# A fused state-space scan and ELU feed-forward kernel: scan bursts, two block turns and the weight sums placed differently

## The chip, the cores and the metric

The kernel runs on one core of a Trainium2 chip. The core has TensorE (matrix products; PE in the profile, its weight loads PEld), VectorE (DVE), ScalarE (ACT), GpSimd (POOL) and SyncE (SP), which issues the transfers. The metric is device time in microseconds (us). The kernel before takes 362.3 us, the median of three runs (361.17 to 363.4).

## The reference

The first half is a Mamba-2 scan with 4 batches, 8 heads, 768 tokens, head width 32 and state width 16, in chunks of tokens. The second is a feed-forward layer with ELU over the 3072 x 256 result:

```python
cum = np.cumsum(np.log(np.clip(a, 1e-6, 1.0)))      # within a chunk
M = (C @ B.T) * exp(cum_i - cum_j) * causal
y = M @ x + (C @ state) * exp(cum)
state = exp(cum_last) * state + sum_j B_j x_j exp(cum_last - cum_j)
...
h = y @ w_in                                   # 3072x256 @ 256x2048
g = np.where(h > 0, h, np.exp(np.minimum(h, 0)) - 1)
out = g @ w_out                                # 3072x2048 @ 2048x256
```

The weights come as 64-bit floating-point numbers; the kernel makes 32-bit ones of their two halves of words.

## The kernel before, in words

**Blocks.** The 3072 tokens are 12 blocks of 256 (BLK). Block n belongs to a batch and a place in it; blocks 2p and 2p + 1 are a pair. Within a block the scan works in quarters of 64 tokens (u, v) and groups of two heads (q).

**The scan of a block** is a chain of steps, each a function: `load_bc` and `load_x` bring B, C and x; `turn` brings B and C into the layout with the state width down the partitions, by four TensorE transposes (L389), a ScalarE copy (L393) and a VectorE product with the mask `hmask2` (L396); `turn_exp` multiplies C by the decay `ec` (L404). From block 6 on the same is done without TensorE: `load_bc` loads B and C in squares and B once more token by token (`b_tok`), and `turn_part` runs, one part at a time, two VectorE transposes of 32 x 32 squares (`turn_square`, L413), the mask (`mask_heads`, L421) and `turn_exp`. `decay` fills L on ScalarE and GpSimd, `scaled` scales B on GpSimd (L379), `scores` are the products C B (L501), `weigh` multiplies them by L (L510), `sums` are the products B x (L531), `states` carries the state on (VectorE, then GpSimd), and `across` (L576) and `inside` (L595) are the products with the state and with M; ScalarE copies their result into yT (L612). The products of `scores`, `sums`, `across` and `inside` are small (32 or 64 rows) and many: a burst in TensorE's stream. For two blocks together `across` and `inside` are 96 products, which stand in the profile as 192 weight loads and 192 products, since each fp32 product is done in two halves.

**The layer.** `l1(n, i)` makes two of 16 column groups of h for block n (L625, four products of 128 x 256), `elu` turns them into g (ScalarE L638 and L645, VectorE L647), `l2(n, j)` adds up the output (L746). Blocks 0 to 3 use these for the first layer. From block 4 on, a pair goes through a seven-product scheme of the Strassen-Winograd kind: the pair's inputs and the weights are summed first (`sum_y` on GpSimd, `sum_weights`), `front`, `mid` and `back` are the seven products of one column group (L697) with VectorE sums between them (`front_sums` L714, then L722 and L730), and `second(n)` is the second layer of a pair, in 56 steps of two products each (L807), with `sum_t1`, `sum_t2` and `add` on GpSimd and VectorE. Its first user is the pair of blocks 2 and 3.

**Order.** Nothing is reordered: each engine does its instructions in the order in which the code issues them, and waits at semaphores. The order is written out by hand:

- a prologue for blocks 0 and 1, then twelve `l1` of blocks 0 and 1 (the loop at L966), with the scan of block 2 between them;
- stages 2 and 3 (the loop at L1082), eight steps each: `l2` of block n - 2, `l1` of block n, its ELU, the conversion of a piece of w_out (`w_take` and `w_give`, in the first six steps of stage 2), and parts of the scans of blocks 3, 4 and 5. In stage 3, `more_sums(i)` makes part i of the sums of both weights (VectorE for w_out, GpSimd for w_in, L673) and the sum `sum_t1` of the pair 2, 3 (L774);
- stages 4, 6, 8 and 10 (the loop at L1122), 16 steps k each, two per column group: even steps `front`, odd ones `mid` and `back`, with steps of `second(n - 2)` between them (`l2s`), and the scan of the next pair. `ends` says at which step the pair's `across` and `inside` come (`end_of_two`), `left` makes what is left of the weight sums, in steps of one VectorE instruction;
- `second` of the last pair, and the stores.

Rotating buffers set further waits: seven PSUM buffers in the pool `ps_a`, two each of `bc`, `b_tok` and `bct`.

Of the kernel before, what the change touches and what calls it, by code (L numbers as in the profile page):

```python
# [16 lines left out]
P = 128  # L17
Q = 64
BLK = 2 * P
# [9 lines left out]
def kernel(  # L29
# [27 lines left out]
    nc = tc.nc  # L57
# [48 lines left out]
    def load_bc(n, c_queue=nc.sync):  # L106
        b, g = place(n)
        st.setdefault(n, {})["bc"] = raw.tile([P, 2, 2, NH, N], F32, tag="bc", name="bc", bufs=2)
        if n > 5:
            st[n]["b"] = raw.tile([P, 2, NH, N], F32, tag="b", name="b_tok", bufs=2)  # L110
            for u in range(2):
                sl = slice((2 * g + u) * P, (2 * g + u + 1) * P)
                nc.sync.dma_start(
                    out=st[n]["b"][:, u], in_=B[b, :, sl, :].rearrange("h s n -> s h n"))


            squares = st[n]["bc"].rearrange("p k u h n -> p k (u h n)").rearrange(
                "p k (m r) -> p k m r", m=2)
            for k, src in enumerate((B, C)):
                for m in range(2):  # L120
                    nc.sync.dma_start(
                        out=squares[:, k, m],
                        in_=src[b, m:NH:2, g * BLK:(g + 1) * BLK, :].rearrange(
                            "q (c t) n -> q c (t n)", t=8))
            return
        for u in range(2):
            sl = slice((2 * g + u) * P, (2 * g + u + 1) * P)
            for k, src in enumerate((B, C)):
                (nc.sync, c_queue)[k].dma_start(
                    out=st[n]["bc"][:, k, u], in_=src[b, :, sl, :].rearrange("h s n -> s h n"))  # L130
# [243 lines left out]
    def scaled(n, eng):  # L374

        s = st[n]
        s["sc"] = sc = att.tile([P, 2, NH, N], F32, tag="sc", name="sc", bufs=2)
        factor = eb0[:, :, NH * n:NH * (n + 1)] if n < 2 else eb[:, :, rows_of(n)]
        eng.tensor_tensor(  # L379
            out=sc, in0=s["b"] if n > 5 else s["bc"][:, 0],  # L380
            in1=factor.unsqueeze(3).to_broadcast([P, 2, NH, N]), op=ALU.mult)

    def turn(n):
# [232 lines left out]

    g_of = {}

    def l1(n, i):

        ps = psum([P, 2, BLK], "ps_h")
        for j in range(2):
            m = 2 * i + j
            for k in range(KC):
                nc.tensor.matmul(  # L625
                    out=ps[:, j], lhsT=w_in[:, k, m * P:(m + 1) * P],
                    rhs=yT[n // 2][:, k, n % 2].rearrange("p u i -> p (u i)"),
                    start=(k == 0), stop=(k == KC - 1))
        lag.append((n, i, ps))

    lag = []
# [334 lines left out]
    for s, (n, i) in enumerate((  # L966
            (1, 0), (1, 1), (1, 2), (0, 4), (1, 3), (0, 5), (1, 4), (0, 6), (1, 5), (0, 7),
            (1, 6), (1, 7))):
        l1(n, i)
        if s < 8:  # L970
            decay_of(2, s)
        if s == 7:
            scores(2)
            weigh(2, 0)
            weigh(2, 1)
        if s % 2 == 1 and todo < 10:
            w_take(todo, nc.vector)
            w_give(todo)
            w_load(todo + 6)
            todo += 1  # L980
        if s == 4:
            scaled(2, nc.gpsimd)
        if s == 5:
            turn(2)
            first_exp(2)
            turn_exp(2)
        if s == 8:
            spread_cum(3)
            load_x(3)
            spread_exp(3)  # L990
            weigh(2, 2)
            weigh(2, 3)

            st[0] = kept
            sums(2, 0, pool=p_o, tag="o", parts=(None, last))
            states(0, last)
            st.pop(0)
            states(2)
        if s == 10:
            spread_cum(4)  # L1000
            inside(across(2), 2)
        if len(lag) > 1:
            elu()


    ends = {(3, 13): (4, 5), (4, 13): (6, 7), (6, 13): (8, 9), (8, 12): (10, 11)}

    def end_of_two(n, step):
        ns = ends.get((n, step))
# [9 lines left out]
    def scan_ahead(n, i):  # L1019


        m = n + 2 + n % 2
        if 4 < m < NP and n % 2 == 1 and i in (4, 5):
            spread_cum(m + i - 4)
        m = n + 2 - n % 2
        if 4 <= m < NP and n % 2 == 0:
            if i < 2:
                if m == 4:
                    load_bc(m + i)
                spread_exp(m + i)  # L1030
            if i == 2:
                if m == 4:
                    spread_cum(5)
                load_x(m)
                load_x(m + 1)
            for k in (i,) if m == 4 else (i, i + 1) if i % 2 == 0 else ():
                if k >= 2:
                    decay(m + k // 6, (k - 2) % 4)
            if m == 4 and i in (5, 7):
                turn(m + i // 7)  # L1040
                turn_exp(m + i // 7)
        if n % 2 == 1 and i in (1, 3) and n + 3 + i // 2 < NP:
            load_bc(n + 3 + i // 2)
        if n == 3 and i > 3 and i < 7:
            turn_part(6, i - 4)
        if 4 <= m < NP and n % 2 == 1:
            if i == 0:
                scaled(m, nc.gpsimd)
                scaled(m + 1, nc.gpsimd)
            for k in (i,) if m == 4 else (i, i + 1) if i % 2 == 0 else ():  # L1050
                if k < 2:
                    decay(m + 1, k + 2)
            if i == 2 and m == 4:
                scores(m, m + 1)
                sums(m, m + 1)
                for q in range(4):
                    weigh(m, q)
                    weigh(m + 1, q)
                states(m)
                states(m + 1)  # L1060
# [15 lines left out]
    def more_sums(i):  # L1076
        sum_weights(nc.vector, a_out, s_out, i)
        sum_weights(nc.gpsimd, a_in, s_in, i)
        sum_t1(2, i, nc.vector)


    for n in (2, 3):  # L1082
        for i in range(8):
            l2(n - 2, i)
            if todo < len(pieces):
                w_take(todo, nc.vector)
# [25 lines left out]
            else:  # L1112
                if i == 0:
                    s_in[:], s_out[:] = weight_sums(), weight_sums()
                elif i < 7:
                    more_sums(i - 1)
            scan_ahead(n, i)
            end_of_two(n, 2 * i + 1)
    sum_t2(2, 0)
    left = (step for i in (6, 7) for step in weight_steps(nc.vector, a_out, s_out, i))  # L1120

    for n in range(4, NP, 2):  # L1122
        m = n + 2 if n + 2 < NP else None
# [13 lines left out]
        for k in range(16):  # L1137
# [16 lines left out]
                    end_of_two(n, k)  # L1154
                    l2s(2)
            elif m and i == 5:
                l2s(1)
                mid(n, i)
                begin_elu()
                states(m)  # L1160
# [5 lines left out]
            else:  # L1166
# [9 lines left out]
                begin_elu()  # L1176
                turn_step(n, k, True)
                if n == 4 and i < 4:
                    for _ in range(2):
                        next(left)()  # L1180
                    if i < 2:
                        sum_weights(nc.gpsimd, a_in, s_in, 6 + i)
                        sum_t1(2, 6 + i)
                l2s(1)
            if m:
                scan_ahead(n + k // 8, k % 8)
                if k == 9:
# [50 lines left out]
```

## Time and profile before

| | |
|---|---|
| timed runs, median (range) | 362.3 us (361.17 to 363.4) |
| the profiled execution, its own time | 363.81 us |
| its span, first to last instruction | 362.1 us |
| granted TensorE clock, mean | 0.993 |
| busy: PE, PEld, DVE, ACT, POOL | 352.8, 315.5, 240.4, 200.8, 232.0 us |
| products of `second` (L807), records x mean | 1120, 275 to 279 ns |
| products of `front`, `mid`, `back` (L697) | 448, 379 to 388 ns |
| products of `l1` (L625) | 256, 383 ns |
| HBM read and written | 22.12 and 3.34 MB |

The mean of a product is the time from its start to its modelled end; products are pipelined, so that the time from start to start is shorter. A row of a timeline or of the chain begins with the start and the length in us; x8 is the number of instructions merged into it; in brackets stands the idle time before it and what ended it. "issue" is time in which the engine waited for nothing that the profile shows.

### The profile page before, as it was taken

To read this page: it belongs to the slowest core of one execution; us is meant where nothing else is said; L and a number is where in the kernel's file an instruction comes from. 1 tells how busy PE (TensorE), PEld (TensorE's weight loads), DVE (VectorE), ACT (ScalarE), POOL (GpSimd) and SP (SyncE) were. 2 spreads that over 40 slices of the span, in tenths; PEclk is the share of its full clock that TensorE was granted. 3 is DMA by queue.
4 is the path that set the end of the run, shared out by engine and by line. 5 is a ranking of instruction groups with operands and counts; after the bars stand their busy time and mean duration, and the time that the engine had idled before them with its cause. 6 is when DMAs were issued, how large, how long until landed. Compare 5 with 4: busy or idle time off the path is not lost.

```text
span 362.1 us, 9921 instructions
## 1 busy us (share of the span) xinstructions
PE 352.8 (97%) x3954; PEld 315.5 (87%) x3954; DVE 240.4 (66%) x495; ACT 200.8 (55%) x493; POOL 232.0 (64%) x368
## 2 busy tenths in 40 slices
PE   8899999999999999999999999999979999999995
PEld 5578888888888998989999989999969999999995
DVE  3989978972699668675777575777564465556212
ACT  4759969767335666545676545676534443535000
POOL 5554544663467996868485968485966445465983
PEclk9999999999999999999999999999998999999999
DMA  8977998652350400155500164500000100000001
GB/s 169 207 206 153 230 292 169 109 81 45 73 119 31 89 0 3 24 119 112 101 0 2 23 129 102 102 3 0 2 2 4 58 2 1 2 0 31 30 2 58
DMA packets 85845, 26.09 MB, mean 72 GB/s; under 512 B 63848, under 2 KB 81704, under 8 KB 85800
## 3 DMA queue, kind: packets, MB, share of 16 engines
q1 hardware_dynamic: 83624, 25.27, 32.0%
q8 instruction: 31, 0.51, 0.6%
q10 hardware_dynamic: 2176, 0.20, 0.4%
q14 instruction: 14, 0.11, 0.1%
HBM read 22.12 MB, written 3.34 MB: 70 GB/s over the span
## 4 chain that ended last, share of the span: by engine, by line
PE 88%; POOL 5%; DVE 4%; issue 1%; ACT 1%; POOLq 0%; DVEq 0%
PE ps_o L807 32%; PE ps_h L697 25%; PE ps_h L625 14%; PE ps_o L746 8%; PE ps_y L595 2%; PE ps_g L501 2%; POOL g L762 2%; PE ps_y L576 1%; PE ps_st L531 1%; PE ps_idle L232 1%; POOL g L774 1%; DVE mag L207 1%; DVE mag L200 1%; POOL w_sum L673 1%; DVE M L510 1%
## 5 line engine op out<-in xcount | busy, mean ns | idle before, releaser
L638 ACT ACTIVATE e<-ps_h 128x512 f32<-128x512 f32 x96 | 57.0, 593 | 92.1 <-DVE ps_h L722 45.4
L807 PEld LDWEIGHTS ps_o<-w_out,g 128*128 128x128 f32 x640 | 80.3, 192 | 3.3 <-issue 0.5
L807 PE MATMUL ps_o<-w_out,g 128*128 128x128 f32 x640 | 81.4, 275 | 0.0
L647 DVE SCALAR_TENSOR_TENSOR g<-e,ps_h 128x512 f32<-128x512 f32 x96 | 65.0, 678 | 15.5 <-ACT e L645 15.1
L625 PE MATMUL ps_h<-yT,w_in 128*128 128x256 f32 x256 | 60.7, 383 | 2.0 <-POOL w_in L217 1.7
L645 ACT ACTIVATE e<-e 128x512 f32<-128x512 f32 x96 | 60.9, 635 | 2.0
L774 POOL TENSOR_TENSOR g<-g 128x256 f32<-128x256 f32 x34 | 25.1, 740 | 55.5 <-DVE g L647 55.5
L625 PEld LDWEIGHTS ps_h<-yT,w_in 128*128 128x128 f32 x256 | 47.7, 190 | 10.3 <-POOL w_in L217 3.1
L807 PE MATMUL ps_o<-w_sum,g 128*128 128x128 f32 x320 | 43.9, 279 | 0.0
L807 PEld LDWEIGHTS ps_o<-w_sum,g 128*128 128x128 f32 x320 | 41.9, 195 | 1.5 <-PE ps_y L595 0.2
L481 ACT ACTIVATE L<-L,ncum 128x64 f32<-128x64 f32 x160 | 41.0, 337 | 0.0
L697 PE MATMUL ps_h<-y_sum,w_sum 128*128 128x256 f32 x128 | 38.8, 384 | 0.5 <-DVE u_sum L714 0.5
L697 PE MATMUL ps_h<-yT,w_in 128*128 128x256 f32 x128 | 39.2, 388 | 0.0
L697 PE MATMUL ps_h<-y_sum,w_in 128*128 128x256 f32 x128 | 38.1, 380 | 0.0
L730 DVE TENSOR_TENSOR ps_h<-ps_h,u_sum 128x512 f32<-128x512 f32 x32 | 22.3, 698 | 23.6 <-PE ps_h L697 23.5
L486 POOL TENSOR_SCALAR_AFFINE_SELECT L<-L 64x512 f32<-64x512 f32 x40 | 28.1, 702 | 13.0 <-ACT L L481 11.7
L722 DVE TENSOR_TENSOR ps_h<-ps_h,u_sum 128x256 f32<-128x256 f32 x32 | 13.8, 431 | 30.5 <-PE ps_h L697 30.1
L714 DVE TENSOR_TENSOR u_sum<-ps_h,u_sum 128x512 f32<-128x512 f32 x32 | 22.0, 687 | 13.3 <-PE ps_h L697 8.0
L746 PE MATMUL ps_o<-w_out,g 128*128 128x256 f32 x128 | 30.8, 383 | 0.0
L762 POOL TENSOR_TENSOR t<-g 128x256 f32<-128x256 f32 x40 | 29.4, 767 | 0.3
L762 POOL TENSOR_TENSOR g<-g,t 128x256 f32<-128x256 f32 x40 | 28.7, 750 | 0.3
L697 PEld LDWEIGHTS ps_h<-y_sum,w_sum 128*128 128x128 f32 x128 | 24.2, 192 | 5.4 <-DVE u_sum L714 2.2
(111 smaller groups left out, 538.3 us busy)
## 6 DMA issues: line engine op xcount, KB each, us to landing
L<-flat SPq DMA_DIRECT2D x20, 256.0 KB, 6.6
w<-in_moe_w_in_dram SPq DMA_DIRECT2D x8, 512.0 KB
w<-in_moe_w_out_dram SPq DMA_DIRECT2D x8, 512.0 KB, 10.4
xr<-in_x_dram SPq DMA_DIRECT2D x24, 128.0 KB, 2.6
out_dram<-c_sum SPq DMA_DIRECT2D x10, 256.0 KB
bc<-in_B_dram SPq DMA_DIRECT2D x24, 64.0 KB, 5.7
bc<-in_C_dram SPq DMA_DIRECT2D x22, 64.0 KB
ec<-flat_exp SPq DMA_DIRECT2D x9, 128.0 KB
```

What stands on the lines that cost most here:

```text
L481: nc.scalar.activation(L[:, h, u], L[:, h, u], ACT.Exp, bias=ncum[:, u, row:row + 1])
L486: nc.gpsimd.affine_select(out=part, in_=part, pattern=[[0, 4], [0, 2], [1, Q]], compare_op=ALU.is_ge, fill=0.0, base=0, channel_multiplier=-1)
L625: nc.tensor.matmul(out=ps[:, j], lhsT=w_in[:, k, m * P:(m + 1) * P], rhs=yT[n // 2][:, k, n % 2].rearrange("p u i -> p (u i)"), start=(k = ...
L638: nc.scalar.activation(begun[0], lag[0][2], ACT.Relu, scale=-1.0)
L645: nc.scalar.activation(e, e, ACT.Exp, scale=-1.0)
L647: nc.vector.scalar_tensor_tensor(out=g_of[n, i], in0=e, scalar=1.0, in1=ps, op0=ALU.subtract, op1=ALU.max)
L697: nc.tensor.matmul(out=out, lhsT=lhsT, rhs=rhs, start=first, stop=True, skip_group_check=True)
L730: nc.vector.tensor_tensor(out=c2, in0=c2, in1=u[:, 0:2], op=ALU.add)
L746: nc.tensor.matmul(out=o_of[n][:, ts], lhsT=g_of[n, j][:, m % 2, ts * P:(ts + 1) * P], rhs=w_out[:, m], start=(m == 0 and ts == 0), stop=( ...
L762: nc.gpsimd.tensor_tensor(out=out, in0=in0, in1=in1, op=ALU.subtract)
L774: eng.tensor_tensor(out=b12, in0=b12, in1=b11, op=ALU.subtract)
L807: nc.tensor.matmul(out=ps[:, ts], lhsT=b[:, ts * P:(ts + 1) * P], rhs=a[:, i], start=(i == chunk[0] and ts == 0), stop=(i == chunk[-1]), s ...
```

## The change

- `l1` takes a number of parts; in the loop at L966 its first two calls (columns 0 and 1 of block 1) are issued with the 256 tokens in two halves, so that each of their products of 128 x 256 is two of 128 x 128.
- Blocks 4 and 5 take the path of the later blocks: loads in squares and `b_tok`, two VectorE transposes each, `mask_heads` and `turn_exp`, spread over steps 3 to 7 of stage 2 and steps 0, 2 and 3 of stage 3. Their TensorE transposes and ScalarE copies go.
- The end of blocks 10 and 11 moves from step 12 to step 13 of stage 8.
- In stage 3, `more_sums(i - 1)` is issued at the start of step i, ahead of that step's `l2`, `l1` and ELU, and for i up to 7; it stood after the ELU, for i up to 6. `left` holds only part 7, one instruction in each of four odd steps of stage 4, and GpSimd's part 6 and its `sum_t1` go from stage 4 into stage 3.
- In stages 4, 6 and 8 one step of `second` goes from step 9 (after `back`) to step 11 (before `mid`).

```diff
     def load_bc(n, c_queue=nc.sync):
-        if n > 5:
+        if n > 3:
             st[n]["b"] = raw.tile([P, 2, NH, N], F32, tag="b", name="b_tok", bufs=2)
...
-            out=sc, in0=s["b"] if n > 5 else s["bc"][:, 0],
+            out=sc, in0=s["b"] if n > 3 else s["bc"][:, 0],
...
-    def l1(n, i):
+    def l1(n, i, parts=1):
         ps = psum([P, 2, BLK], "ps_h")
         for j in range(2):
             m = 2 * i + j
-            for k in range(KC):
-                nc.tensor.matmul(
-                    out=ps[:, j], lhsT=w_in[:, k, m * P:(m + 1) * P],
-                    rhs=yT[n // 2][:, k, n % 2].rearrange("p u i -> p (u i)"),
-                    start=(k == 0), stop=(k == KC - 1))
+            for part in range(parts):
+                toks = slice(part * BLK // parts, (part + 1) * BLK // parts)
+                for k in range(KC):
+                    nc.tensor.matmul(
+                        out=ps[:, j, toks], lhsT=w_in[:, k, m * P:(m + 1) * P],
+                        rhs=yT[n // 2][:, k, n % 2].rearrange("p u i -> p (u i)")[:, toks],
+                        start=(k == 0), stop=(k == KC - 1))
...
-        l1(n, i)
+        l1(n, i, 2 if s < 2 else 1)
...
-    ends = {(3, 13): (4, 5), (4, 13): (6, 7), (6, 13): (8, 9), (8, 12): (10, 11)}
+    ends = {(3, 13): (4, 5), (4, 13): (6, 7), (6, 13): (8, 9), (8, 13): (10, 11)}
...
-            if m == 4 and i in (5, 7):
-                turn(m + i // 7)
-                turn_exp(m + i // 7)
+            if m == 4 and i > 2:
+                turn_part(m + i // 6, i % 3)
...
-        if n == 3 and i > 3 and i < 7:
+        if n == 3 and i == 0:
+            turn_part(5, 2)
+        if n == 3 and i in (2, 3):
+            turn_part(i + 2, 3)
+        if n == 3 and i in (4, 5, 6):
             turn_part(6, i - 4)
...
     for n in (2, 3):
         for i in range(8):
+            if n == 3 and i > 0:
+                more_sums(i - 1)
             l2(n - 2, i)
...
                 if i == 0:
                     s_in[:], s_out[:] = weight_sums(), weight_sums()
-                elif i < 7:
-                    more_sums(i - 1)
...
-    left = (step for i in (6, 7) for step in weight_steps(nc.vector, a_out, s_out, i))
+    left = weight_steps(nc.vector, a_out, s_out, 7)
...
             elif m and i == 5:
-                l2s(1)
+                l2s(2)
                 mid(n, i)
...
                 if n == 4 and i < 4:
-                    for _ in range(2):
-                        next(left)()
-                    if i < 2:
-                        sum_weights(nc.gpsimd, a_in, s_in, 6 + i)
-                        sum_t1(2, 6 + i)
-                l2s(1)
+                    next(left)()
+                    if i == 0:
+                        sum_weights(nc.gpsimd, a_in, s_in, 7)
+                        sum_t1(2, 7)
+                if not m or i != 4:
+                    l2s(1)
```

## The prediction

> **What bounds the kernel.** I read the page first (busy shares, slices, chain), then the waits of TensorE, then the chain in order of time, then the timelines of TensorE and VectorE around what stood out.
>
> ```profile
> PE 352.8 (97%) x3954; PEld 315.5 (87%) x3954; DVE 240.4 (66%) x495; ACT 200.8 (55%) x493; POOL 232.0 (64%) x368
> ...
> PE   8899999999999999999999999999979999999995
> ...
> PEclk9999999999999999999999999999998999999999
> ...
> q8 instruction: 31, 0.51, 0.6%
> ```
>
> TensorE is busy 97% and no other engine over 66%. One slice after the ramp falls to 7, the slice from 262.5 us, and the next one is the only one with a lower clock. The waits of TensorE name few causes:
>
> ```profile
> PE ps_y L595 <- issue: 1.8, 1, 1.8
> ...
> PE ps_h L697 <- DVE u_sum L714: 0.5, 1, 0.5
> ...
> PEld ps_h L697 <- DVE u_sum L714: 2.2, 5, 0.9
> ```
>
> So what can be won is TensorE's own work and these few gaps. The chain by time shows the big one:
>
> ```profile
> 171.79 1.30 PE ps_h L697 x6
> ...
> 226.09 1.30 PE ps_h L697 x6
> ...
> 266.70 0.89 PE ps_o L807 x8
> 269.48 1.81 issue
> 271.30 1.07 PE ps_y L595 x54
> 272.37 2.00 PE ps_o L807 x8
> ...
> 284.17 1.30 PE ps_h L697 x6
> ```
>
> 171.79, 226.09 and 284.17 are the first `front` of stages 6, 8 and 10. Stage 6 lasts 54.30 us, stage 8 58.08, with the same work but for 16 product records fewer in `sums` (0.86 against 0.72 us). Inside the burst of `across` and `inside` of blocks 10 and 11 TensorE waits 1.81 us for nothing but instructions, and right after it eight products take 2.00 us instead of 0.89. The window view has the cause of the second:
>
> ```profile
> 268.59:272.00 3.41, 1.59 (x133) 1.36 (x130) 0.56 (x2) 0.70 (x2) 2.82 (x4) 1.00 0.02 5
> 272.00:275.41 3.41, 3.41 (x37) 3.01 (x20) 0.00 (x0) 1.51 (x5) 2.42 (x4) 0.50 0.02 5
> ```
>
> (columns: stretch, its length, busy time of PE, PEld, DVE, ACT, POOL, then PEclk, DMA share, GB/s.) For 3.41 us the clock is halved.
>
> The instruction queue's packets tell where bursts run dry. Its 31 packets are 16,384 bytes each; TensorE has 8,011 records (each fp32 product of the program is two weight loads and two products). The wait at 269.27 comes before record 6593, the smaller one at 51.2 us (L625, 0.39 us) before record 1473: 5120 apart, 20 blocks of 256. So block starts lie at 193 + 256k, and in the quiet parts a packet starts from 2.5 us before to 1.1 us after TensorE enters the block ahead of it. The two-block bursts hold some 384 records in 2.4 us. The bad one begins 14 records after a block start, so 2.6 us later it needs the next block. That fetch began 2.28 us after the block was entered (why so late the trace doesn't show: no other packet moves then), took 0.93, and the record ran 1.43 us after it landed: 4.64 in all.
>
> **What the Trainium skill says.** "Runtime: NRT & Kernel Launch", Instruction fetch mechanics: instructions are refilled in blocks of 16 KiB, 256 instructions, and the crossing is mostly hidden. The trace agrees on size and count; hidden it is in 29 of 31. The same section gives TensorE room for 128 KiB; here the block needed was fetched only one block ahead. "TensorE: Matmul & The Clock Gate", Part 1: the clock halves after a window of about 3.4 us without enough activity. Here it did so for 3.41 us after a gap of 2 us inside a burst[...]. "VectorE: DVE Perf Modes", The three transpose paths: VectorE turns 32x32 blocks only, into SBUF. The trace has it at 638 ns for 128x256, which is why blocks 4 and 5 now need loads in squares and a second, token-wise load of B.
>
> **The change, part by part.** The sum is made against the profiled execution, 363.81 us (span 362.1 and 1.7 around it).
>
> *A, end of blocks 10 and 11 one step later.* It moves by 14 products, 56 records, and takes `sum_y` (four on POOL) with it; the next `front` is still two steps (6.15 us) away, as in stages 4 and 6. Counting the new order, the four two-block bursts begin 63, 59, 71 and 83 records after a block start (52, 47, 59 and 14 before): 8 products more are 32 records, 8 transposes less are minus 16, the rest are semaphore waits. At 0.11 us a record ahead of the burst the last is 83 x 0.11 + 1.1 = 10 us between block starts, and the shortest of the others 59 x 0.11 + 1.2 = 7.7, more than 4.64. The stall and the half clock go: 58.08 - 54.30 + 0.14 = 3.9. Minus 3.9.
>
> *B, blocks 4 and 5 turned by VectorE.*
>
> ```profile
> 75.45 0.38 PE L389 MATMUL ps_tb<-ident,bc 128*128 128x128 f32 x2
> 75.67 0.38 PE L389 MATMUL ps_tc<-ident,bc 128*128 128x128 f32 x2
> 75.89 1.89 PE L746 MATMUL ps_o<-w_out,g 128*128 128x256 f32 x8
> ```
>
> Each turn holds TensorE 0.44 us (75.45 to 75.89, again 84.22 to 84.66): minus 0.88. VectorE gains four squares (start to start 0.5), and two masks of 0.93 for 0.68: 2.5 us in all; ScalarE loses two copies (0.36 each), which nobody waited for. In stage 2 it has no idle until 79 us, so the last weight piece, which POOL finishes at 79.08, comes 1.0 later, 80.1; its `l2` starts at 80.67 - 0.44 = 80.23. Free, with 0.1 to spare; up to 0.3 if not. SP issues four loads more, about 2.4 us, ahead of x loads that end at 75.4 and are needed at 96; block 6's B waits for POOL's `scaled` at 88 and is needed at 109. Both nothing.
>
> *C, halved products.* 16 records at 216 ns (1.73 for eight) become 32 at 111 (1.78 for sixteen): plus 0.1. They move the block starts early too: record 1473 now falls 26 records before the end of block 2's burst, 0.8 us sooner. With the packet as before the wait grows by 0.9; with the packet 1.3 us earlier, since its block is entered sooner, it vanishes (minus 0.4). I take plus 0.3.
>
> *D, weight sums a step ahead.* Two things meet on VectorE where stage 4 begins:
>
> ```profile
> 118.25 0.69 DVE L647 SCALAR_TENSOR_TENSOR g<-e,ps_h 128x512 f32<-128x512 f32 x1 [0.37 <-PE ps_h L697]
> 118.86 0.68 DVE L714 TENSOR_TENSOR u_sum<-ps_h,u_sum 128x512 f32<-128x512 f32 x1
> ...
> 120.27 0.59 PE L697 MATMUL ps_h<-y_sum,w_sum 128*128 128x256 f32 x2
> ```
>
> The product at 120.27 waits for the sum that ends at 119.54: 0.7 to spare. Queued by hand with the durations of before (sums 2.3 to 2.9 for five, ELU 0.6, weighing 2.65, states 1.7), VectorE now has sums 0 and 1 in its idle time before 96 us, and from 100.9 on sums 2 to 6, five ELUs, two squares, a mask and a `cts`: the last ELU starts about 117.9 and `u_sum` ends at 119.2, against a product that is due at 119.5. The sums of part i - 1 wait for the products of step i - 1, which have read those weights; behind them stands the ELU of step i, and TensorE needs its buffer two steps later at the soonest. I take 0.2 lost, between 0 and 1. What it buys: POOL has one part of the sums less after 120 us and does it before `t`, so that the partial sum that VectorE awaited at 135.68 (1.30 us, POOL) comes 2 us sooner, and TensorE's gap at 138.5 (0.63) goes. Together minus 0.4.
>
> *E, one `l2` step from step 9 to step 11.* At 208.2 and twice more the second product of `mid` follows `u_sum` with one step (0.44) and one product between, and comes 0.14 late, with 0.10 more for the restart. One step more covers it: 3 x 0.24, minus 0.7. At step 9 nothing is uncovered, since the scores' buffers were freed by ELUs a step earlier.
>
> Sum: -3.9 - 0.9 + 0.1 + 0.3 - 0.4 - 0.7 = -5.5, so 358.3. The profiled execution lies 0.4 above the slowest timed run and 1.5 above the median (362.3), which a clock window that falls differently could explain. With the stall gone only the smaller offset should remain: 358.0, 1.2% under the median. About 1% is what this measurement can tell from no change.
>
> **Rivals.**
> 1. The dry fetch is not where but when: a late fetch meets another burst, or record 1473 costs its whole 1.3 us and a halved window (3.41 / 2 = 1.7): 358 + 3 = 361. For: the lateness at 268.93 has no visible cause. Against: the new distances exceed 4.64 everywhere else.
> 2. VectorE becomes the bound in stage 3. It is nine tenths busy from 99 to 117 us. If all seven groups take 2.9 as the last did rather than 2.45, it is 3.1 late, less 0.3 to spare: 360.8.
> 3. Slower: block starts lie otherwise than I count, within 40 records ahead of three or more bursts. Each then costs what blocks 10 and 11 cost now, 3.9; three make 358 + 11.7 = 369.7. It decides when my count is off by 20 to 60 records. Against: it rests on two stalls 20 blocks apart.
>
> The halving and the moves do stand in the built order, so that the change is not what it says is no case.
>
> **Numbers.** Forecast 0.63, rivals 0.18, 0.12, 0.07. Of the forecast nine tenths end under 358.7, plus a little of rival 2: faster 0.62; the rest of 1 and 2: same 0.31; slower 0.07. The range 356.4 to 361.4 takes in C and D at both ends and the first two rivals.
>
> **What would show it.** No issue wait over 0.3 us at an L595 after 60 us and no half clock after the ramp (A); stages of equal length; no L389 transposes for blocks 4 and 5 (B); no gap near 137 us (D); no `u_sum` wait after `sums` (E). Wrong if a PE wait on `u_sum` near 119 us exceeds 1 us, or an instruction wait stands in another burst.

## The result and the profile after

The changed kernel takes 357.8 us (median of four runs, 357.64 to 359.08) against 362.2 us for the kernel before beside it (361.17 to 363.4): the ratio is 0.9885, with a 95% interval from 0.9847 to 0.9923. A second measurement of it ("after, once more" in the table below, experiment 9) gave 357.8 us again. The profiled execution took 357.64 us with a span of 355.9 us, 6.2 us less than the one before. That is more than the medians show (4.4 us), and experiment 1 says why.

The page of the kernel after, its busy shares, the slices of TensorE and of its clock, and its instruction queue:

```profile
PE 349.0 (98%) x3962; PEld 313.4 (88%) x3962; DVE 242.5 (68%) x500; ACT 200.5 (56%) x491; POOL 231.8 (65%) x367
...
PE   8899999999999999999999999999999999999995
...
PEclk9999999999999999999999999999999999999999
...
q8 instruction: 31, 0.51, 0.6%
```

The 7 in the slices of TensorE and the 8 in those of the clock are gone, with the same 31 instruction packets. The waits of TensorE after (total us, times, longest us) are down to two lines, both from the ramp; no instruction wait and no wait for `u_sum` is left in them. In the list of the weight loads (PEld), one wait for `u_sum` of 0.2 us is left of the five:

```profile
PE ps_h L627 <- POOL w_in L217: 1.7, 3, 1.1
PE ps_idle L232 <- DVE idle L227: 1.1, 1, 1.1
...
PEld ps_h L699 <- DVE u_sum L716: 0.2, 1, 0.2
```

The chain of the kernel after, in order of time, with the first `front` of stages 6, 8 and 10 and the last two-block burst:

```profile
169.94 1.30 PE ps_h L699 x6
...
224.00 1.30 PE ps_h L699 x6
...
270.07 1.44 PE ps_y L595 x90
...
277.86 1.30 PE ps_h L699 x6
```

Stage 8 lasts 53.86 us where it lasted 58.08. The burst of blocks 10 and 11 (`inside`, L595) runs through in one piece of 1.44 us.

For all kernels below, the stages were also measured one way: from the first of the 64 products of a stage that read `y_sum` to that of the next. The first column of times says when stage 4 begins, which holds all that happens in the ramp and in stages 2 and 3. From there in stage 10 to the end of TensorE's last product it is 73.93 us in all of them.

| kernel | median us | stage 4 begins | stage 4 | stage 6 | stage 8 |
|---|---|---|---|---|---|
| before | 362.2 | 117.19 | 54.87 | 54.30 | 58.08 |
| after | 357.8 | 116.32 | 53.90 | 54.06 | 53.85 |
| after, once more | 357.8 | 116.69 | 53.90 | 54.06 | 53.85 |
| 1 before, once more | 362.5 | 118.35 | 54.91 | 54.30 | 55.92 |
| 2 only the end moved | 359.9 | 116.79 | 55.05 | 54.30 | 54.08 |
| 3 only products halved | 360.0 | 116.99 | 54.90 | 54.36 | 54.41 |
| 4 after, all twelve halved | 371.3 | 121.15 | 58.34 | 58.16 | 54.54 |
| 5 after, halves undone | 358.9 | 117.58 | 53.89 | 54.06 | 53.84 |
| 6 after, end undone | 358.0 | 116.72 | 53.89 | 54.06 | 54.17 |
| 7 after, sums undone | 359.2 | 116.34 | 54.92 | 54.06 | 53.84 |
| 8 after, l2 step undone | 359.0 | 116.95 | 54.13 | 54.33 | 54.08 |
| 10 after, turns undone | 359.0 | 118.48 | 53.90 | 54.25 | 53.89 |
| 11 after, three halved | 358.3 | 116.25 | 53.90 | 54.06 | 53.85 |

Where no instruction wait falls into them and nothing in them was changed, the stages repeat to 0.2 us, so they are the sharper measure. The start of stage 4 doesn't: the kernel before alone gave 117.19 and 118.35. Nor do the medians from row to row: experiments 1 to 4, 5 to 8 and 9 to 11 ran on three different chips, each group beside the kernel before, whose runs at the full clock had medians of 362.2, 362.1 and 363.0 us there. Only 10 and 11 stand beside the changed kernel (9). A difference of up to 1 us between the median of another row and 357.8 can be the chip's. In the group of 5 to 8, four of the seven runs of the kernel before had the half clock (experiment 1), which put its median at 364.3 us and makes the ratios given there too low.

### The profile page after: what moved, and what is told of

Its sections match the earlier page's. It is cut to its first block, busy times and chain, and to the rows that moved or that the text cites. A ratio compares the mean times of both kernels' runs of the same rounds, so it can differ in the third digit from the quotient of the medians.

```text
span 355.9 us, 9943 instructions
## 1 busy us (share of the span) xinstructions
PE 349.0 (98%) x3962; PEld 313.4 (88%) x3962; DVE 242.5 (68%) x500; ACT 200.5 (56%) x491; POOL 231.8 (65%) x367
## 4 chain that ended last, share of the span: by engine, by line
PE 93%; DVE 3%; ACT 1%; POOL 1%; issue 0%; POOLq 0%; DVEq 0%
PE ps_o L809 35%; PE ps_h L699 28%; PE ps_h L627 14%; PE ps_o L748 8%; PE ps_y L595 2%; PE ps_g L501 2%; PE ps_y L576 1%; PE ps_st L531 1%; PE ps_idle L232 1%; DVE mag L207 1%; DVE mag L200 1%; DVE M L510 1%; DVE sgn L192 0%; DVE g L649 0%; POOL w_in L217 0%; ACT L L471 0%
## 5 line engine op out<-in xcount | busy, mean ns | idle before, releaser
L627 PE MATMUL ps_h<-yT,w_in 128*128 128x256 f32 (+1 forms) x272 | 60.9, 371 | 1.7 <-POOL w_in L217 1.7
L776 POOL TENSOR_TENSOR g<-g 128x256 f32<-128x256 f32 x33 | 23.9, 726 | 54.4 <-DVE g L649 54.4
L809 PE MATMUL ps_o<-w_sum,g 128*128 128x128 f32 x320 | 42.9, 275 | 0.0
L809 PEld LDWEIGHTS ps_o<-w_sum,g 128*128 128x128 f32 x320 | 41.1, 192 | 1.2
L699 PE MATMUL ps_h<-yT,w_in 128*128 128x256 f32 x128 | 38.8, 385 | 0.0
L764 POOL TENSOR_TENSOR g<-t,g 128x256 f32<-128x256 f32 x40 | 27.9, 730 | 1.1 <-PE ps_o L809 1.1
```

The source lines that it names most:

```text
L627: nc.tensor.matmul(out=ps[:, j, toks], lhsT=w_in[:, k, m * P:(m + 1) * P], rhs=yT[n // 2][:, k, n % 2].rearrange("p u i -> p (u i)")[:, toks],
L699: nc.tensor.matmul(out=out, lhsT=lhsT, rhs=rhs, start=first, stop=True, skip_group_check=True)
L764: nc.gpsimd.tensor_tensor(out=out, in0=in0, in1=in1, op=ALU.subtract)
L776: eng.tensor_tensor(out=b12, in0=b12, in1=b11, op=ALU.subtract)
L809: nc.tensor.matmul(out=ps[:, ts], lhsT=b[:, ts * P:(ts + 1) * P], rhs=a[:, i], start=(i == chunk[0] and ts == 0), stop=(i == chunk[-1]), s ...
```

## The experiments

The first four put the cause of the long stage 8 to the test, four more undo one part of the change each in the changed kernel (a fifth follows as experiment 10), and two look at the ramp.

### 1. The kernel before, once more

No edit.

> The kernel before once more, without any edit. If the late fetch in the burst of blocks 10 and 11 is a property of where instruction blocks start in TensorE's stream, the profile has it again: an instruction wait of 1.5 to 2.5 us at an L595 near 270 us, stage 8 longer than stage 6 by 3.5 to 4.2 us, and a time within 0.5% of 362.2 us. If it was the chance of one execution, stage 8 is about 54.5 us here and the half clock is gone.

Median 362.5 us, ratio 1.000 (0.998 to 1.002). TensorE's timeline in the burst of blocks 10 and 11, and the clock slices of this execution:

```profile
268.72 1.24 PE L576 MATMUL ps_y<-cts,Sx 32*64 32x64 f32 x64
269.89 0.79 PE L595 MATMUL ps_y<-M,xr 64*32 64x64 f32 x56
271.95 0.96 PE L595 MATMUL ps_y<-M,xr 64*32 64x64 f32 x72 [1.27 <-issue]
...
PEclk9999999999999999999999999999999999999999
```

The instruction wait is there again, after the same 56 products of `inside`, but with 1.27 us where the first execution had 1.81, just under the range I gave, and with no half clock behind it. So stage 8 is 1.62 us longer than stage 6 here and was 3.78 us longer there. The wait belongs to the kernel; the half clock comes with it only sometimes. The granted clock of each timed run shows how often: of 70 runs of the kernel before, 27 have a mean clock of 0.989 to 0.995 and a median of 364.0 us, 43 have 0.998 or more and a median of 362.2. The difference, 1.8 us, is about half of the 3.41 us window. Of 48 timed runs of the kernels 2, 3 and 5 to 11, one is at a clock under 0.996, and so is one of the four of the changed kernel above (0.993, its slowest, 359.08 us); no profile of these two runs tells where.

The length of the wait need not be all that decides. In experiment 4, where the clock is halved three times, it changes at 116.15, 170.76 and 228.79 us: 16.0 and 17.0 times 3.413 us apart, as if on a fixed grid. In the execution of experiment 1 it changes once, after the last product, at 360.34 us; 26 such steps earlier is 271.60 us, which lies inside the wait. TensorE's busy time in the two stretches that share the wait stands behind the comma in each row:

```profile
268.18:271.60 3.42, 2.49 (x126) 2.00 (x125) 2.07 (x5) 0.96 (x3) 2.30 (x6) 1.00 0.02 5
271.60:275.01 3.41, 3.06 (x87) 2.86 (x87) 0.11 (x1) 1.84 (x5) 2.75 (x4) 1.00 0.02 5
```

That is 0.73 and 0.90 of a stretch, where the kernel before had its whole wait in one (268.59 to 272.00, busy 1.59 us, 0.47), and the half clock in the next. So a wait may bring the half clock or not by where it falls on the grid, which lies differently in every execution: whole in one stretch, this one would have left TensorE busy for 0.63 of it (1 - 1.27 / 3.41, an estimate). Whether that is little enough no run shows, nor that this parts the 27 runs from the 43: only two of the kernel's executions were profiled.

This is why the two profiles differ by more than the medians do: the profiled execution before was one of those with the half clock.

### 2. The end of blocks 10 and 11 alone

```diff
-    ends = {(3, 13): (4, 5), (4, 13): (6, 7), (6, 13): (8, 9), (8, 12): (10, 11)}
+    ends = {(3, 13): (4, 5), (4, 13): (6, 7), (6, 13): (8, 9), (8, 13): (10, 11)}
```

> Only the end of blocks 10 and 11 one step later; its burst now begins 71 records after a block start instead of 14. Theory (where the block starts fall): the instruction wait and the half clock of that burst go, stage 8 falls from 58.1 to 54.3 us, and the time falls by 3.9 us, to 358.3. Rival (the end a step later hands its sums on late, or other work waits): the wait stays or a wait on y_sum or w_sum stands before the first front of stage 10, 360 to 362.5 us. Rival (the profiled execution was an exceptional one, half of them have no half clock): 2 us less, 360.

359.9 us, ratio 0.9921 (0.9891 to 0.9951): 2.7 us less. Stage 8 is 54.08 us, 4.0 us under the first profile and 1.84 under the second. The mechanism is the theory's; the time is the second rival's (360), and the two don't exclude each other: the theory's 3.9 us was the size in an execution with the half clock. Against the 32 runs of the kernel before beside it, 12 of them at the half clock, the end is worth 2.7.

### 3. The halved products alone

```diff
-        l1(n, i)
+        l1(n, i, 2 if s < 2 else 1)
```

(with `l1` taking its parts as in the change)

> Only the halving of the first eight groups of first-layer products, which adds 32 product records (64 records of the stream with their loads counted singly for each pass) some 200 us ahead of the burst of blocks 10 and 11, and leaves that burst and everything near it as it was. Theory (block starts): the burst now begins 46 records after a block start, so its wait goes although nothing of its own work, waits or transfers has changed: minus 3.9, minus 0.4 for the short wait at 51 us, plus 0.3 for the halves: 358.2 us. Rival (the wait has to do with what runs in that burst, with transfers or with semaphores): it stays, and the kernel is 0.1 to 0.3 us slower than before, 362.5 us.

The expectation miscounts its edit: it is that of the change, two calls of `l1` whose 16 product records become 32, so that the stream grows by 32 records with the weight loads, not by 64. The 46 is right. 360.0 us, ratio 0.9928 (0.9906 to 0.9949). The chain of this kernel around the burst, whose own step, work and transfers are those of the kernel before:

```profile
225.98 1.30 PE ps_h L699 x6
...
268.65 1.44 PE ps_y L595 x90
...
280.39 1.30 PE ps_h L699 x6
```

An edit that adds 32 records some 230 us earlier takes the wait out of this burst: it runs its 1.44 us in one piece, and stage 8 falls to 54.41 us. The burst now begins 46 records after a block start instead of 14. That settles it: the wait is a matter of where the blocks of 256 records fall in the stream. The rival, slower by 0.1 to 0.3 us, is out.

Stage 8 is still 0.33 us longer than in experiment 2. The timelines of TensorE have that in one place, `across` of blocks 10 and 11. In experiment 3, at the old step:

```profile
267.41 1.24 PE L576 MATMUL ps_y<-cts,Sx 32*64 32x64 f32 x64
268.58 1.51 PE L595 MATMUL ps_y<-M,xr 64*32 64x64 f32 x128
```

and in experiment 2, a step later:

```profile
271.26 0.91 PE L576 MATMUL ps_y<-cts,Sx 32*64 32x64 f32 x64
272.10 1.51 PE L595 MATMUL ps_y<-M,xr 64*32 64x64 f32 x128
```

The difference is a wait that the lists of waits leave out as too short. In the middle of the slow `across` TensorE starts nothing from 267.71 to 267.94 us. GpSimd makes the states `Sx` that these products read (L553). The timelines of GpSimd and of the weight loads have, in experiment 3,

```profile
266.89 0.99 POOL L553 TENSOR_TENSOR Sx<-S_new,hmask 128x64 f32<-128x64 f32 x3 [1.69 <-DVE S_new L548]
...
267.94 0.57 PEld L576 LDWEIGHTS ps_y<-cts,Sx 32*64 32x64 f32 x40
```

and that of GpSimd in experiment 2

```profile
266.78 1.00 POOL L553 TENSOR_TENSOR Sx<-S_new,hmask 128x64 f32<-128x64 f32 x3 [1.69 <-DVE S_new L548]
```

The last `Sx` is done at 267.88 us in experiment 3, and the weight load that waits for it starts within 0.06 us. In experiment 2 it is done 3.5 us before the burst begins. So the old step comes too early for the states of these blocks, and this wait is apart from the instruction wait: experiments 3 and 6 have it without an instruction wait, and experiment 4 has instruction waits without it.

### 4. All twelve calls halved

```diff
-        l1(n, i, 2 if s < 2 else 1)
+        l1(n, i, 2)
```

> The changed kernel with the remaining ramp products halved too, which moves the block starts on by about 160 records: every one of the four bursts of two blocks then holds two block starts, some 1.6 us apart, where a fetch took about 3.2 us from the entry of its block to the first instruction of the next. Theory: an instruction wait of about 1.6 us in each of the four bursts, each with up to 1.7 us more for a halved clock, and about 1.2 us for the halves themselves: 357.8 + 8 to 15 = 366 to 373 us. Rival (the place of block starts doesn't matter): plus 1.2 us alone, 359 us.

371.3 us (368.27 to 372.34), ratio 1.022 (1.015 to 1.029) against the kernel before, 13.5 us over the changed kernel. The waits of TensorE and the clock slices:

```profile
PE ps_y L595 <- issue: 7.5, 4, 2.7
...
PEclk9999999999998999998999998999999999999999
```

and its timeline in the second of the four bursts:

```profile
166.93 1.24 PE L595 MATMUL ps_y<-M,xr 64*32 64x64 f32 x99
170.91 0.67 PE L595 MATMUL ps_y<-M,xr 64*32 64x64 f32 x29 [2.74 <-issue]
171.51 0.79 PE L699 MATMUL ps_h<-yT,w_in 128*128 128x256 f32 x1
```

Four waits, one in each two-block burst, where they had been put: 1.99, 2.74, 2.36 and 0.45 us. The first three are followed by the half clock, three slices at 8; a single product of `front` right after takes 0.79 us. They sum to 7.5 us, and three halved windows to 3 x 3.41 / 2 = 5.1; the span is 14.1 us longer than after's, which leaves 1.5 for the halves themselves and for TensorE's restarts after the waits. A wait of about 1.6 in each was expected, so the first three were undersized, the second by 1.1, and the fourth oversized. The 3.2 us that the expectation counts from block to block were 2.20 to 4.59 (table of experiment 6).

The stretches of 3.41 us that hold the four waits, on the grid of this execution:

```profile
112.74:116.15 3.41, 1.42 (x61) 1.19 (x53) 3.28 (x8) 1.62 (x5) 0.72 (x1) 1.00 0.02 5
167.35:170.76 3.41, 0.82 (x72) 0.66 (x65) 0.76 (x2) 1.59 (x4) 3.41 (x6) 1.00 0.56 115
225.38:228.79 3.41, 1.06 (x90) 0.84 (x77) 1.20 (x3) 1.59 (x4) 3.32 (x5) 1.00 0.65 131
283.40:286.81 3.41, 2.96 (x137) 2.58 (x135) 0.75 (x2) 2.92 (x8) 3.41 (x6) 1.00 0.02 5
```

TensorE was busy for 0.42, 0.24 and 0.31 of the three that a half clock followed, and for 0.87 of the fourth.

### 5. The halves undone

```diff
-        l1(n, i, 2 if s < 2 else 1)
+        l1(n, i)
```

> The changed kernel with the first-layer products whole again: the four bursts of two blocks begin 31, 27, 39 and 51 records after a block start instead of 63, 59, 71 and 83. Theory: a burst runs dry only if the time from the entry of one block to the next (records ahead of the burst at 0.11 us, the rest at 0.0063) is under what a fetch took, 3.2 us (good ones) to 4.64 us (the bad one). Here that is 4.8, 4.4, 5.7 and 6.9 us, so no wait or one of at most 0.3 us in the second burst; 0.3 us less for the whole products, the short wait at 51 us back with 0.2 to 0.5 us: 357.6 to 358.1 us. Rival (the halves are what keeps the bursts fed): waits of 1 us or more in the first two bursts, 360 us or more.

358.9 us (358.22 to 359.67). Nothing waits in the four bursts and all stages have their length: with the turns on VectorE and the end a step later, the halves aren't needed there. The time is nevertheless 1.1 us over the 357.8 of the changed kernel, which ran on another chip (ratio to the kernel before 0.9877, 0.9810 to 0.9944): above my range, and not for the rival's reason. TensorE's waits and then its timeline show where 0.8 of it is:

```profile
PE ps_h L627 <- ACT yT L612: 1.9, 1, 1.9
...
PE ps_h L627 <- issue: 0.8, 1, 0.8
```

```profile
51.33 0.91 PE L627 MATMUL ps_h<-yT,w_in 128*128 128x256 f32 x3
53.01 1.24 PE L627 MATMUL ps_h<-yT,w_in 128*128 128x256 f32 x5 [0.77 <-issue]
```

It is record 1473, after the burst of block 2, in the ramp. If the halves are worth anything, it lies there. That this one wait explains the median isn't shown, since the start of stage 4 moves by more than that from run to run.

### 6. The end undone

```diff
-    ends = {(3, 13): (4, 5), (4, 13): (6, 7), (6, 13): (8, 9), (8, 13): (10, 11)}
+    ends = {(3, 13): (4, 5), (4, 13): (6, 7), (6, 13): (8, 9), (8, 12): (10, 11)}
```

> The changed kernel with the end of blocks 10 and 11 back at its old step: that burst begins 26 records after a block start, 4.3 us from block to block. Theory: with the products halved the old step would do almost as well, a wait of 0 to 0.4 us in that burst, 357.8 to 358.3 us. Rival (the old step is bad for its own sake, whatever the stream): the burst waits again for 1 us or more, 359.5 to 361.5 us.

358.0 us (357.61 to 358.39; ratio 0.9852, 0.9797 to 0.9907), as the theory had it. The timeline of TensorE: the burst runs in one piece, with the slow `across` of experiment 3 again.

```profile
265.59 1.24 PE L576 MATMUL ps_y<-cts,Sx 32*64 32x64 f32 x64
266.76 1.51 PE L595 MATMUL ps_y<-M,xr 64*32 64x64 f32 x128
```

So the old step costs 0.32 us in stage 8 for its own sake, and the instruction wait is gone by the other parts' shift of the stream alone. Part A and part C each suffice to take it away, and neither is worth it twice.

The packets of the instruction queue put the runs side by side. The block is the one whose start lies ahead of the burst of blocks 10 and 11, except in experiment 4, where it is the block that starts inside each of the four bursts. The packets were matched to the blocks by their order; times in us.

| run | block start, records ahead of the burst | packet starts, from the block's entry | next block's first record runs, from the entry | wait |
|---|---|---|---|---|
| before | 14 | +2.28 | 4.65 | 1.81 |
| 1 | 14 | +1.72 | 4.10 | 1.27 |
| 6 | 26 | -1.61 | 3.72 | none |
| 3 | 46 | -2.19 | 5.28 | none |
| 5 | 51 | -2.61 | 4.95 | none |
| 2 | 71 | -1.46 | 5.88 | none |
| after | 83 | -1.62 | 7.03 | none |
| 4, first | 33 inside | +1.09 | 3.72 | 1.99 |
| 4, second | 37 inside | +1.82 | 4.59 | 2.74 |
| 4, third | 25 inside | +1.29 | 4.09 | 2.36 |
| 4, fourth | 13 inside | -0.18 | 2.20 | 0.45 |

The distance between block starts isn't all. With 26 records or more of ordinary work ahead of the burst, the packet in this table starts 1.5 to 2.6 us before TensorE enters the block (0.1 to 4.4 us ahead of the other two-block bursts of all runs but 4), and the next block has landed before the burst needs it. With 14, or with the start inside a burst, it mostly starts 1.1 to 2.3 us after the entry. In experiment 6 TensorE needs the next block 3.72 us after the entry, sooner than in the kernel before, and doesn't wait. What the rows with a wait have in common is the landing: in all six the record that waited ran 1.34 to 1.50 us after the packet had landed, and in the rows without one 4.3 us or more lay between. So it is the packet that these waits wait for; what sets the moment at which a packet starts stays open.

### 7. The weight sums undone

```diff
-            if n == 3 and i > 0:
-                more_sums(i - 1)
...
+                elif i < 7:
+                    more_sums(i - 1)
...
-    left = weight_steps(nc.vector, a_out, s_out, 7)
+    left = (step for i in (6, 7) for step in weight_steps(nc.vector, a_out, s_out, i))
...
-                    next(left)()
-                    if i == 0:
-                        sum_weights(nc.gpsimd, a_in, s_in, 7)
-                        sum_t1(2, 7)
+                    for _ in range(2):
+                        next(left)()
+                    if i < 2:
+                        sum_weights(nc.gpsimd, a_in, s_in, 6 + i)
+                        sum_t1(2, 6 + i)
```

> The changed kernel with the weight sums at their old places, one step later. Theory: the wait on u_sum at the start of stage 4 (0.5 us) and the gap at 138.5 us (0.6 us) are back, and only stage 4 is longer, by 0.9 us: 358.7 us. Rival (the stage grew shorter for another reason, the turns or the l2 step): stage 4 stays at 53.9 us and the time at 357.8.

359.2 us (358.7 to 360.61; ratio 0.9891, 0.9832 to 0.9949); stage 4 is 54.92 us, 1.02 longer, and the others are as in the changed kernel. The time lies 0.5 us above the expected 358.7. The wait stands at 138 us and not at the start of the stage. The timeline of TensorE in experiment 7:

```profile
137.44 0.60 PE L699 MATMUL ps_h<-yT,w_in 128*128 128x256 f32 x2
138.60 0.70 PE L699 MATMUL ps_h<-y_sum,w_sum 128*128 128x256 f32 x2 [0.56 <-DVE u_sum L716]
```

and in the changed kernel:

```profile
137.41 0.60 PE L699 MATMUL ps_h<-yT,w_in 128*128 128x256 f32 x2
137.84 0.59 PE L699 MATMUL ps_h<-y_sum,w_sum 128*128 128x256 f32 x2
```

From one start to the next it is 1.16 us against 0.43: 0.73, and 0.10 more for the restart (the second of the two products follows late). Another 0.15 us of the stage lies at `mid` near 154 us, where the second product waits for `u_sum` again, in spite of the moved `l2` step. The expectation wrongly counted one wait as two: the 0.5 us in the list of waits is this gap.

### 8. The l2 step undone

```diff
             elif m and i == 5:
-                l2s(2)
+                l2s(1)
...
-                if not m or i != 4:
-                    l2s(1)
+                l2s(1)
```

> The changed kernel with the l2 step back from step 11 to step 9. Theory: stages 4, 6 and 8 are each 0.24 us longer, a restart of TensorE before the second product of mid in each: 358.5 us. Rival: with VectorE freed by the earlier weight sums, its u_sum comes in time anyhow and the stages keep their length, at least stage 4: 357.8 to 358.3.

359.0 us (358.71 to 359.51; ratio 0.9881, 0.9826 to 0.9936). Stages 4, 6 and 8 are 0.23, 0.27 and 0.23 us longer: the theory. The timeline of TensorE at `mid` in stage 4 with the step undone:

```profile
153.10 0.60 PE L699 MATMUL ps_h<-yT,w_in 128*128 128x256 f32 x2
153.67 0.70 PE L699 MATMUL ps_h<-y_sum,w_sum 128*128 128x256 f32 x2
```

The second product starts 0.57 us after the first instead of 0.43. The list of the products' waits doesn't show it; the start-to-start times do, and the list of the weight loads has four waits for `u_sum` with 1.3 us in all, against one of 0.2 in the changed kernel. The median is 1.2 us over the changed kernel's; 0.4 us of that stands in a short instruction wait at record 1473, and it isn't the step's.

### 9 and 11. The changed kernel once more, and three calls halved

Experiment 9 has no edit; 11 is

```diff
-        l1(n, i, 2 if s < 2 else 1)
+        l1(n, i, 2 if s < 3 else 1)
```

> The changed kernel once more. It shows how far stage lengths, the short wait at record 1473 and the time up to stage 4 differ from run to run: stages 4, 6 and 8 within 0.1 us of 53.9, 54.06 and 53.85, the first front of stage 4 anywhere between 116.0 and 117.2 us, a median of 357.8, half a microsecond either way.

> The changed kernel with one more step of first-layer products halved, three instead of two: record 1473 comes 42 records before the end of block 2's burst instead of 26, its block's predecessor is entered some 0.8 us earlier, and the four long bursts begin 79, 75, 87 and 99 records after a block start. Theory: the wait at record 1473, which was 0 to 0.5 us in runs of the changed kernel's stream, is gone for good: minus 0.2 on the mean, plus 0.15 for the halves: no difference, 357.8 us. Rival (a start nearer the end of that burst comes later in its own time, so more records are needed sooner): a wait of 0.5 to 1 us there, 358.5 us.

9: 357.8 us (357.42 to 358.63), ratio 0.9855 (0.983 to 0.988); the stages are the same to 0.01 us. The list has no wait at record 1473, but the record starts 0.25 us after the one ahead of it, which is a wait too short for the list. 11: 358.3 us (357.59 to 358.72), ratio 0.9866 (0.9841 to 0.9890); no instruction wait in its list either, and the intervals overlap widely. The theory (357.8) and the rival (358.5) lie too close together for the medians to part them, but the rival's wait isn't in the profile. Nothing beyond the change is shown to be won by it.

### 10. The turns undone

```diff
-        if n > 3:
+        if n > 5:
...
-            if m == 4 and i > 2:
-                turn_part(m + i // 6, i % 3)
+            if m == 4 and i in (5, 7):
+                turn(m + i // 7)
+                turn_exp(m + i // 7)
...
-        if n == 3 and i == 0:
-            turn_part(5, 2)
-        if n == 3 and i in (2, 3):
-            turn_part(i + 2, 3)
-        if n == 3 and i in (4, 5, 6):
+        if n == 3 and i > 3 and i < 7:
```

(and the factor of `scaled` as before)

> The changed kernel with blocks 4 and 5 turned by TensorE again (the four bursts then begin 84, 79, 91 and 103 records after a block start, all harmless). Theory: TensorE has the two turns of 0.44 us back near 75 and 84 us, no stage changes its length: plus 0.9 us, 358.7. Rival (VectorE was near its limit in stage 3 and the squares cost there what TensorE won): stage 3 gets shorter by as much, no difference, 357.8.

359.0 us (358.53 to 359.91), ratio 0.9889 (0.9867 to 0.9911): 1.2 over the changed kernel run beside it. The timeline has the two turns back:

```profile
76.74 0.38 PE L389 MATMUL ps_tb<-ident,bc 128*128 128x128 f32 x2
76.96 0.38 PE L389 MATMUL ps_tc<-ident,bc 128*128 128x128 f32 x2
77.17 1.89 PE L748 MATMUL ps_o<-w_out,g 128*128 128x256 f32 x8
```

Between 60 us and stage 4 the lag behind the changed kernel grows by 0.44 and 0.44 at the turns, shrinks by 0.08 between them, and doesn't change in stage 3: the rival is out, the squares cost TensorE nothing. A step of 0.19 us in stage 6 comes with a block whose first record ran 1.41 us after its packet had landed, as soon after it as in the waits of the table above. The rest of the difference lies ahead of the turns, in the ramp; between this profile and the changed kernel's first one, 0.7 us of it lie at record 1473.

## Why the prediction was right, and where it was off

The direction and the main cause were right: 358.0 forecast, 357.8 measured. That the time came out to 0.2 us is luck: the terms were less exact than that, and two errors cancel.

| step | forecast | measured | from |
|---|---|---|---|
| A end of blocks 10 and 11 | -3.9 | -4.0 | stage 8, 58.08 to 53.85, less 0.23 of E |
| B turns by VectorE | -0.88 | -0.8 | lag at the turns, before against after |
| C the halves themselves | +0.1 | +0.30 | chain, 10.63 to 10.93 us |
| C record 1473 | +0.3 | -0.4 | wait of 0.39 us gone |
| D weight sums | -0.4 | -0.73 | lag at 138 us, before against after |
| E l2 step | -0.7 | -0.70 | 0.23 + 0.24 + 0.23 |
| sum | -5.5 | -6.3 | the profiled executions: -6.2 |

The terms add up to 0.2 more than the two executions differ by because 0.16 us more pass after TensorE's last product, 3.88 us against 3.72. The terms up to stage 4 (B and C) were read at their places, since the start of stage 4 as such moves by more than they are worth.

**A** held in mechanism and size, against the profile it was made from. It holds 1.71 us of half clock (3.41 / 2), 0.33 of the slow `across`, a wait for the states that I hadn't seen, and 1.96 of the instruction wait (58.08 less 54.41, less 1.71). What failed is the step from the profile to the median. I put the difference between the profiled execution and the median of before (1.5 us) to a clock window "that falls differently", and subtracted 0.3 of it. It was the half clock itself, which six runs in ten of the kernel before don't have; the changed kernel's profile then lies 0.2 under its median and not 0.3 above. So 363.81 - 5.5 - 0.3 = 358.0 met 363.81 - 6.2 + 0.2 = 357.8: gains undersized by 0.7, an offset wrong by 0.5 the other way. A sum against the median needs A at 2.7 us (experiment 2); with the other terms as forecast it gives -4.3, 358.0 as well.

The rule in A, distances of block starts against 4.64 us, gave the right answer for every burst by wrong numbers. The distances were overestimated (10 us for the last burst, and the packets show 7.0), and the fetch that must fit starts before the block is entered where ordinary work lies ahead. In experiments 5 and 6 as little as 3.38 us (second burst of 5) and 3.72 us (last of 6) lay between two entries, well under 4.64, and nothing waited.

**B** held. VectorE's extra work came to 0.25 us on the last weight piece (its last step starts at 77.29 us after, 77.04 before), not to 1.0, because the conversion's own steps around the two squares were shorter (0.41 us where they had been 0.51 in the last piece, 0.64 where it had been 1.12 in the first step of the piece ahead); why was not tried. Rival 2, VectorE as the bound in stage 3, didn't come about: it was 47.4 us busy of the 57 from 63 to 120 us (43.7 before), and `u_sum` ended at 118.66 us against a product at 119.40.

**C** was mis-sized twice. The chain has the halves in one row of the kernel after, and the product that waited in another:

```profile
27.76 10.93 PE ps_h L627 x64
...
51.04 1.94 PE ps_h L627 x8
```

Before, the first was 10.63 us with 48 products; 16 more cost 0.30 and not 0.1. The eight products of the second took 2.32 us before, in pieces of three and five with the wait between. I chose plus 0.3 between -0.4 and +0.9, and in this execution the lower end came: the packet came 1.07 us sooner (48.14 us, 49.21 before), as the lower bound said it might. In experiments 6 and 8, with the same stream up to there, it came too late, and the record waited 0.5 and 0.4 us; in 7 it came in time, and in 9 it was 0.24 us late. So the term is a draw of every run. Counted from start to start, the record waits 0 to 0.67 us in the seven profiles with these halves (0.37 in the mean) and 0.37 to 0.93 in the four without them (0.58). The 0.21 between the means is less than the 0.30 that the halves cost, so no gain of the halves themselves is shown; what they did for certain, in experiment 3, is to move the block starts.

**D** was undersized because of the 0.2 us that I took off for the wait at 119 us, which doesn't occur, and because the restart after the gap (0.10) wasn't counted. The gap before, in TensorE's timeline, where the second row starts 1.07 us after the first:

```profile
138.28 0.60 PE L697 MATMUL ps_h<-yT,w_in 128*128 128x256 f32 x2
139.35 0.70 PE L697 MATMUL ps_h<-y_sum,w_sum 128*128 128x256 f32 x2 [0.47 <-DVE u_sum L714]
```

**E** held to 0.02.

**Rivals.** Rival 1, a late fetch elsewhere, didn't show after 60 us in the profiles of the changed kernel; experiment 4 shows what it would have cost. Rival 3 turned on my count of block starts. The four waits of experiment 4, at the places that the count gave, and the missing one of experiment 3 say that the count is right.

## What to carry to other kernels

Where an engine runs long bursts of very short instructions, a page that names "issue" as the releaser of a wait should be read as a question of the instruction stream: count records, look at the packets of the instruction queue, and see where the block starts fall. Here 32 records added some 230 us ahead took such a wait away, and 160 more brought four of them, and the code of the burst says nothing of it; so a comparison of two kernels should look at this before it puts a gain or a loss down to the edit. A term read from one profiled execution has to be asked whether the other runs have it too; the granted clock of each run answered that here. And a step that is a little slow without an entry in the list of waits can still hold a wait: start-to-start times and the engine that makes the input showed one of 0.3 us.

## What the runs showed of the hardware that wasn't expected

- The half clock followed waits of 1.81, 1.99, 2.36 and 2.74 us inside bursts of small products, and not those of 1.27 and 0.45 us. The Trainium skill, "TensorE: Matmul & The Clock Gate", Part 1, speaks of an idle window of about 3.4 us; the window of reduced clock agrees (3.41 us), but the one ahead of it needn't be idle: TensorE was busy for 0.24 to 0.47 of it. In all the other such windows between 14 and 350 us, in all the profiles, it was busy for 0.73 or more, and the full clock followed. What happens between 0.47 and 0.73 is not shown.
- The instruction packets in the table of experiment 6 start up to 2.6 us before their block is entered or up to 2.3 us after. In the ramp, with the weights being loaded, a packet starts 1.5 to 4.6 us after the entry at all of the blocks 193, 449, 1217 and 1473. Whether the loads cause that was not tried.
